# A transformer block on one core: wider steps in the first MLP product, thirteen shared buffers, another order of the residual's statistics, fewer opening products

## The chip, the cores and the metric

The kernel runs on one core of one Trainium2 chip. The time is device microseconds of one execution, and a kernel is judged by the median of several executions. The engines that matter here are PE (TensorE, matrix products), DVE (VectorE), ACT (ScalarE), POOL (GpSimd) and SP (SyncE, which here only issues transfers). Each has a queue of its own, and they wait for each other through semaphores.

## The reference

One sequence of 2048 tokens, width D = 576, 32 heads of 18 features, MLP width 4608:

```python
    def _A_ref(x, wqkv, w_phi, wo):
        ...
        phi_q = jnp.concatenate([_softmax(pq, axis=-1), _softmax(-pq, axis=-1)], axis=-1)
        phi_k = jnp.concatenate([_softmax(pk, axis=-1), _softmax(-pk, axis=-1)], axis=-1)
        kv = jnp.einsum("bhsf,bhsd->bhfd", phi_k, v)
        z  = jnp.einsum("bhsf->bhf", phi_k)
        num = jnp.einsum("bhqf,bhfd->bhqd", phi_q, kv)
        den = jnp.einsum("bhqf,bhf->bhq", phi_q, z)[..., None] + 1e-6
        o = num / den
        return (...)(o, 0, 2, 1, 3).reshape(B, S, D) @ wo
    def _B_ref(x, w1, b1, w2, b2):
        y = _layernorm(x, axis=-1)
        h = _gelu(jnp.einsum("bsd,df->bsf", y, w1) + b1)
        return jnp.einsum("bsf,fd->bsd", h, w2) + b2
    x = A_x
    h = x + _A_ref(_layernorm(x, axis=-1), A_wqkv, A_w_phi, A_wo)
    h2 = h + _B_ref(_layernorm(h, axis=-1), B_w1, B_b1, B_w2, B_b2)
```

So there is a layer norm, a linear attention with softmax features, a residual, a second layer norm, and an MLP with a second residual. All inputs are bf16.

## The kernel before, in words

The 2048 tokens are 16 tiles of 128, taken as 8 pairs. `NS` is 8 and `TB` is 256: one pair of tiles. The order of every engine's instructions is the order in which the source issues them (`manual_schedule` over all five engines), so a line that stands earlier in the source stands earlier in its engine's queue. Nothing is planned by a cost model.

**The front** (L705 to L1053) is a list of calls written out by hand. It opens with `warm(20)`: twenty products of the identity with 512 columns, whose result nobody reads. It folds the feature weights into the query and key weights (`flip_mm`, `fold_k_mm`, with casts on ACT by `fold_k_ev`), copies half of the value weights to the other partitions on POOL (`copy_values`, L162), and runs keys, values and queries for all pairs. Query features are kept as `phiq`, eight buffers.

**The MLP** is eight blocks, `mlp(s_)` for `s_` in 0 to 7, each over one pair of tiles:

- `up` is the first product. Its contraction over 576 is cut into nine steps of two halves of 64 rows. The two matmuls of a step take separate halves of the array and run side by side. One `pair(...)` is 18 matmuls (nine steps) of 256 columns into two PSUM buffers of the pool `acc` (six buffers). Eighteen pairs make one `up`, 324 matmuls on L1075. ACT applies GELU to both buffers (L1096) and writes `h`.
- `down` is the second product: per tile and half of the output 36 matmuls of 288 columns (L1117), 144 in a block. DVE adds the bias and residual (L1121), and a transfer on SP writes the tile out.
- Between them stands what feeds later blocks. `norm_q` sums and divides the query features (DVE L460 and L462, POOL L466); `turn_q` transposes them by two transfers on SP (L494) into `phiT`; `combine` makes ten matmuls on them (L588) and a division on DVE (L598, L601); `turn` transposes the result (L618) into `oT`; `enter` does the attention's output product (36 matmuls, L635), the residual and its statistics on DVE (L648, L649), the second normalisation (POOL L239, DVE L243), and transposes each tile (L677) into `ln2T`, the moving operand of a later `up`.

`at` holds calls that are issued at a given pair of `up` or at a given matmul of `down`. In the block `s_ = 1`, `norm_q` of pair 3 ends and `turn_q(3)` follows at pair step 3 of `up`; `enter(2)` follows `up`; `combine(6)` stands at matmul 30 of `down`, `leave(3)` (that is `combine(7)` and `turn(3)`) at 76, and the two halves of `norm_q(4, ...)` at 90 and 110. The later blocks do the same one pair further on, as long as pairs remain.

`ln2T` is two buffers of 256 tokens that alternate. The MLP's `h` takes the four buffers of `lnt_pool`, `phiq` and `phiT` rotate through nine of `ex_pool`.

Of the kernel before, what the change touches and what calls it, by code (L numbers as in the profile page):

```python
# [8 lines left out]
P = 128  # L9
# [13 lines left out]
NM = FF // P  # L23
# [16 lines left out]
def kernel(  # L40
# [82 lines left out]
    def region(at, n):  # L123
        return shared[:, at : at + n]
# [9 lines left out]
    ln2T = [  # L134
        region(4 * PW + i * KC * TB, KC * TB).rearrange("p (c t) -> p c t", c=KC)
        for i in range(2)
    ]
# [121 lines left out]
    def chunks(t):  # L259
        return xh[:, t, :].rearrange("p (c k) -> p c k", k=KH)  # L260

    lnT = [
        lnt_pool.tile([P, 2, KC, P], BF16, name="lnT", tag="lnT") for _ in range(NT // 4)
    ]
    moments = {}

# [182 lines left out]

    def query_exp(p, i):  # L450
        if p not in phiq:
            phiq[p] = ex_pool.tile([P, 2, PW], BF16, name="phiq", tag="ex")
        exponentials("q", phiq[p], p, i)

    def part_of(dst, i):
# [33 lines left out]
            query_weigh(p, i, a, pool)  # L489

    def turn_q(p):
        phiT[p] = ex_pool.tile([P, 2, KC, P], BF16, name="phiT", tag="ex")
        for a in range(2):
            nc.sync.dma_start_transpose(phiT[p][:, a, :, :], phiq[p][:, a, :])  # L494

    left = list(range(NT))

# [73 lines left out]
        )  # L571

    products = {}

    def combine_mm(t, part=None, home=None):
        p, a = divmod(t, 2)
        if not part:
            products[t] = (home or pn_pool).tile(
                [P, 2, 512], FP32, name="pn", tag="two" if home else "pn"
            )  # L580
        pn = products[t]
        for w in range(*((0, KC) if part is None else ((0, 5), (5, KC))[part])):
            h0, h1 = FIRST[w], FIRST[w] + COUNT[w]
            for b in range(2):
                lo, hi = max(h0, b * HH), min(h1, (b + 1) * HH)
                if lo >= hi:
                    continue
                nc.tensor.matmul(  # L588
                    pn[:, b, (lo - b * HH) * VW : (hi - b * HH) * VW],
                    phiT[p][:, a, w, :], kvm[:, w, (lo - h0) * VW : (hi - h0) * VW],  # L590
                    start=(w == 0 or (b == 1 and lo == HH)),
                    stop=(w == KC - 1 or (b == 0 and hi == HH)), skip_group_check=True,
                )

    def divide(t):
        rec = small.tile([P, 2, HH], FP32, name="rec", tag="rec")
# [42 lines left out]
        flight["a", p, i] = pa  # L639

    def residual_add(p, i, a):
        if (p, a) not in gathered:
            gathered[p, a] = small.tile(
                [P, 2, nc.vector.BN_STATS_DIM], FP32, name="st2", tag="st2"
            )
        t = 2 * p + a
        cs = slice(i * HALF, (i + 1) * HALF)
        nc.vector.tensor_tensor(xh[:, t, cs], flight["a", p, i][a], xh[:, t, cs], ALU.add)  # L648
        nc.vector.bn_stats(gathered[p, a][:, i, :], xh[:, t, cs])  # L649

    def second(t):
        p, a = divmod(t, 2)
# [4 lines left out]
    def residual(p, banks):  # L657
        for i in range(2):
            residual_mm(p, i, banks())
            for a in range(2):  # L660
                residual_add(p, i, a)
                if i:
                    second(2 * p + a)

# [5 lines left out]
        return ln2[t % 2][:, :, :, :].rearrange("p c two k -> p (c two k)")  # L670

    def place2(t):
        s_, i_ = divmod(t, TPS)
        return ln2T[s_ % 2][:, :, i_ * P : (i_ + 1) * P]

    def turn2(t):
        nc.sync.dma_start_transpose(place2(t), rows2(t))  # L677
# [332 lines left out]
    query_mm(1, 0)  # L1010
    residual_mm(0, 1, double_bank())
    residual_add(0, 1, 0)
    residual_add(0, 1, 1)
    query_exp(1, 0)
    query_mm(6, 1)
    query_exp(6, 1)
# [3 lines left out]
    query_mm(1, 1)  # L1020
    query_exp(1, 1)
    residual_add(0, 0, 0)
    second(0)
    residual_add(0, 0, 1)
    close_keys()
    query_mm(2, 1)
    second(1)
# [24 lines left out]
    close_weights()  # L1052
    load_w2(0, 3)  # L1053
    hb_pool = side_pool("hb_pool", 1)
    tt_pool = side_pool("tt_pool", 1)
    psA.close()

    acc = ctx.enter_context(
# [5 lines left out]
            acc.tile([P, HALF], FP32, name="pa", tag="acc")[:, :] for _ in range(2)  # L1064
        ]

    def up(s_, at, first=0):
        x = ln2T[s_ % 2]
        h1 = [lnt_pool.tile([P, KC, TB], BF16, name="h1", tag="lnT") for _ in range(4)]

        def pair(ph, p_, cols):
            for c in range(KC):
                for half in range(2):
                    rows = slice(half * KH, (half + 1) * KH)
                    nc.tensor.matmul(  # L1075
                        ph[half][:, cols],
                        w1[p_ // 9][rows, c, p_ % 9 * P : (p_ % 9 + 1) * P], x[rows, c, cols],
                        start=(c == 0), stop=(c == KC - 1),
                    )

        def banks_of():
            return [acc.tile([P, TB], FP32, name="ph", tag="acc") for _ in range(2)]

        begun = [banks_of() for _ in range(first)]
        for p_ in range(first):
            pair(begun[p_], p_, slice(0, P))
            if p_ == 0:
                yield
        for p_ in range(NM // 2):
            if p_ in at:  # L1090
                at[p_]()
            ph = begun[p_] if p_ < first else banks_of()
            pair(ph, p_, slice(P if p_ < first else 0, TB))
            for half in range(2):
                m = p_ + half * NM // 2
                nc.scalar.activation(  # L1096
                    h1[m // 9][:, m % 9, :], ph[half][:, :], AF.Gelu_apprx_tanh,
                    bias=b1col[:, m : m + 1], scale=1.0,
                )
        yield h1  # L1100

    def down(s_, h1, at):
        k = 0
        for i_ in range(TPS):
            t = s_ * TPS + i_
            hb = hb_pool.tile([P, D], FP32, name="hb", tag="hb")
            nc.gpsimd.tensor_tensor(hb[:, :], xh[:, t, :], b2bc[:, :], ALU.add)  # L1107
            ot = tt_pool.tile([P, D], BF16, name="ot", tag="ot")
            for i in range(2):
                cs = slice(i * HALF, (i + 1) * HALF)  # L1110
                po = acc.tile([P, HALF], FP32, name="po", tag="acc")
                for n in range(NM):
                    m = n // 2 + n % 2 * NM // 2
                    if k in at:
                        at[k]()
                    k += 1
                    nc.tensor.matmul(  # L1117
                        po[:, :], h1[m // 9][:, m % 9, i_ * P : (i_ + 1) * P], w2[m // 18][:, m % 18, cs],
                        start=(n == 0), stop=(n == NM - 1),
                    )  # L1120
                nc.vector.tensor_tensor(ot[:, cs], po[:, :], hb[:, cs], ALU.add)  # L1121
            nc.sync.dma_start(out_v[:, t, :], ot[:, :])

    def enter(a):
        residual(a, two_banks)
# [6 lines left out]
        combine(2 * p + 1)  # L1132
        turn(p)

    def mlp(s_):
        a, b, c = s_ + 1, s_ + 2, s_ + 3
        rises, falls = {}, {}
        if s_ == 0:
            rises = {
                6: lambda: [load_w2(1, n) for n in range(6)],  # L1140
                15: lambda: combine(2 * a),
                17: lambda: turn_q(b),
            }
        if s_ == 1:
            rises[3] = lambda: (norm_q(b, 1), turn_q(b))
        rise = up(s_, rises, 1 if s_ == 0 else 0)
        if s_ == 0:
            turn2_mm(1, pn_pool)
            next(rise)
            for part in range(2):  # L1150
                turn2_ev(1, part, dve)
            for q in (a, b):
                for i in range(2):
                    norm_q(q, i)
                if q == a:
                    turn_q(q)
        h1 = next(rise)
        if s_ == 0:
            falls = {
                0: lambda: leave(a), 64: lambda: enter(a), 84: lambda: combine(2 * b),  # L1160
                96: lambda: norm_q(c, 0), 118: lambda: leave(b),
            }
        else:
            if a < NS:
                enter(a)
            if b < NS:
                falls[30] = lambda: combine(2 * b)
                falls[76] = lambda: leave(b)
            if c < NS:
                falls[90] = lambda: norm_q(c, 0)  # L1170
                falls[110] = lambda: (norm_q(c, 1), turn_q(c))
        down(s_, h1, falls)

    for s_ in range(NS):
        mlp(s_)
    ordered.close()


# [28 lines left out]
```

## Time and profile before

| what | value |
|---|---|
| median of 3 runs | 400.38 us (400.46, 400.38, 397.94) |
| the profiled execution's own time | 397.7 us |
| its span | 396.0 us |
| PE busy | 386.7 us, 98% of the span |
| PE's share of the chain that ended last | 92% |
| granted clock of PE | 1.0 |

The page gives busy time by engine, the span in 40 slices, the chain of work that ended last (followed back from the last instruction), and groups of instructions by line and shape. Mean times of single matmuls include the overlap with their neighbours. The duration of a stretch in the chain, divided by its count, is therefore the better measure of what one matmul costs. In the timeline a row merges neighbours of one kind; PEld is the loading of weights for a matmul, which runs beside PE.

### The profile page before, as it was taken

To read this page: it belongs to the slowest core of one execution; us is meant where nothing else is said; L and a number is where in the kernel's file an instruction comes from. 1 tells how busy PE (TensorE), PEld (TensorE's weight loads), DVE (VectorE), ACT (ScalarE), POOL (GpSimd) and SP (SyncE) were. 2 spreads that over 40 slices of the span, in tenths; PEclk is the share of its full clock that TensorE was granted. 3 is DMA by queue.
4 is the path that set the end of the run, shared out by engine and by line. 5 is a ranking of instruction groups with operands and counts; after the bars stand their busy time and mean duration, and the time that the engine had idled before them with its cause. 6 is when DMAs were issued, how large, how long until landed. Compare 5 with 4: busy or idle time off the path is not lost.

```text
span 396.0 us, 12120 instructions
## 1 busy us (share of the span) xinstructions
PE 386.7 (98%) x5424; PEld 318.2 (80%) x5424; DVE 163.7 (41%) x347; ACT 186.6 (47%) x399; POOL 124.0 (31%) x148
## 2 busy tenths in 40 slices
PE   8899999889999999999999999999999999999996
PEld 4687777679878888888888888888887888778874
DVE  5999894485248026403630462065107200600000
ACT  3978887678500850184028303820481058007700
POOL 7999998019004203400340133023202100211010
PEclk9999999999999999999999999999999999999999
DMA  8999869998924605510460053005300400210000
GB/s 221 190 173 175 196 113 165 213 238 222 280 48 84 99 2 76 74 33 2 80 81 22 3 102 78 4 2 105 78 2 18 89 17 2 41 37 17 2 17 15
DMA packets 72163, 33.83 MB, mean 85 GB/s; under 512 B 58786, under 2 KB 69296, under 8 KB 72112
## 3 DMA queue, kind: packets, MB, share of 16 engines
q1 hardware_dynamic: 71760, 32.75, 41.9%
q8 instruction: 42, 0.69, 0.7%
q10 hardware_dynamic: 288, 0.30, 0.3%
q14 instruction: 9, 0.07, 0.1%
q0 software_dynamic: 64, 0.02, 0.0%
HBM read 16.53 MB, written 2.36 MB: 48 GB/s over the span
## 4 chain that ended last, share of the span: by engine, by line
PE 92%; POOL 3%; DVE 2%; DMA 1%; issue 1%; POOLq 0%
PE ph L1075 36%; PE po L1117 36%; PE pk L409 7%; PE pa L635 4%; PE pv L409 4%; PE acc_kv L503 2%; PE pn L588 2%; DMA w<-in_A_w_phi_dram 1%; POOL wv L162 1%; POOL vals L209 1%; POOL rs L285 1%; PE pW L379 0%; DVE shared L243 0%; POOL w L201 0%; DVE ob L601 0%
## 5 line engine op out<-in xcount | busy, mean ns | idle before, releaser
L1096 ACT ACTIVATE h<-ph,b1col 128x256 bf16<-128x256 f32 x288 | 120.7, 470 | 166.9 <-PE ph L1075 149.0
L1117 PE MATMUL po<-w,h 128*128 128x288 bf16 x1152 | 144.7, 287 | 0.0
L1075 PE MATMUL ph<-shared,w 64*128 64x256 bf16 (+1 forms) x2610 | 143.3, 269 | 0.0
L1075 PEld LDWEIGHTS <-w 64*128 64x128 bf16 x2610 | 127.6, 94 | 15.0 <-issue 1.7
L1117 PEld LDWEIGHTS <-h 128*128 128x128 bf16 x1152 | 111.2, 98 | 29.3 <-issue 1.9
L239 POOL TENSOR_TENSOR rs<-va,mhalf 128x1 f32<-128x1 f32 x16 | 8.8, 549 | 171.4 <-DVE va L237 171.4
L648 DVE TENSOR_TENSOR xh<-pa,xh 128x288 bf16<-128x288 f32 x32 | 14.3, 447 | 114.9 <-PE pa L635 114.9
L409 PEld LDWEIGHTS <-lnT 64*128 64x128 bf16 x864 | 42.0, 94 | 10.4 <-issue 0.3
L1121 DVE TENSOR_TENSOR ot<-po,hb 128x288 bf16<-128x288 f32 x32 | 14.6, 456 | 80.5 <-PE po L1117 79.7
L466 POOL TENSOR_TENSOR phiq<-phiq,rk 128x576 bf16<-128x576 bf16 x32 | 36.4, 1162 | 21.6 <-DVE rk L462 16.3
L1107 POOL TENSOR_TENSOR hb<-xh,b2bc 128x576 f32<-128x576 bf16 x16 | 20.4, 1273 | 62.8 <-DVE ot L1121 61.1
L466 POOL TENSOR_TENSOR phik<-phik,rk 128x576 bf16<-128x576 bf16 x32 | 36.4, 1163 | 1.7 <-PE pv L409 0.9
L460 DVE TENSOR_REDUCE sk<-phik 128x64 f32<-128x1152 bf16 x16 | 21.2, 1323 | 5.2 <-ACT phik L431 5.2
L431 ACT ACTIVATE phiq<-pk 128x576 bf16<-128x576 f32 x32 | 18.7, 650 | 6.6 <-PE pk L409 6.6
L460 DVE TENSOR_REDUCE sk<-phiq 128x64 f32<-128x1152 bf16 x16 | 21.3, 1334 | 0.2 <-ACT phiq L431 0.2
L409 PE MATMUL pv<-wv,lnT 64*128 64x288 bf16 x288 | 20.6, 283 | 0.1
L431 ACT ACTIVATE phik<-pk 128x576 bf16<-128x576 f32 x32 | 18.8, 653 | 3.2 <-PE pk L409 3.2
L409 PE MATMUL pk<-shared,lnT 64*128 64x288 bf16 x288 | 19.8, 283 | 0.0
L409 PE MATMUL pk<-wqp,lnT 64*128 64x288 bf16 x288 | 19.7, 283 | 0.0
L635 PE MATMUL pa<-wo,shared 64*128 64x288 bf16 x288 | 19.1, 283 | 0.0
L462 DVE RECIPROCAL rk<-sk 128x64 f32<-128x64 f32 x32 | 17.7, 553 | 1.5
L635 PEld LDWEIGHTS <-shared 64*128 64x128 bf16 x288 | 14.0, 94 | 3.6 <-issue 0.2
(70 smaller groups left out, 194.5 us busy)
## 6 DMA issues: line engine op xcount, KB each, us to landing
w<-in_B_w_dram SPq DMA_DIRECT2D x24, 432.0 KB, 7.9
out_dram<-ot SPq DMA_DIRECT2D x16, 144.0 KB, 1.7
xh<-in_A_x_dram SPq DMA_DIRECT2D x3, 576.0 KB, 6.9
wo<-in_A_wo_dram SPq DMA_DIRECT2D x4, 324.0 KB, 6.4
wv<-in_A_wqkv_dram SPq DMA_DIRECT2D x2, 324.0 KB, 8.4
w<-in_A_wqkv_dram SPq DMA_DIRECT2D x4, 157.5 KB, 9.5
wqp<-wqp SPq DMA_DIRECT2D x2, 288.0 KB, 3.9
w<-in_A_wqkv_dram SPq DMA_DIRECT2D x1, 322.0 KB, 4.9
```

Of the source, the lines that this page charges most:

```text
L409: nc.tensor.matmul(dst[:, a, 0:HALF], lhs[rows, c, :], w[rows, slot, i * HALF : (i + 1) * HALF], start=(n == 0), stop=(n == KC - 1),)
L431: nc.scalar.activation(rows[:, :, i * HH : (i + 1) * HH, s, :], flight[key, p, i][:, :, 0:HALF].rearrange("p a (h f) -> p a h f", f=DH), A ...
L460: nc.vector.tensor_reduce(sk[:, :, :], part_of(dst, i), AX.X, ALU.add)
L462: nc.vector.reciprocal(rk[:, :, :], sk[:, :, :])
L466: eng.tensor_tensor(part, part, flight["r" + key, p, i][:, a, :].rearrange("p (h o) -> p h o", o=1).to_broadcast([P, NH, DH]), ALU.mult,)
L635: nc.tensor.matmul(pa[a], oT[p % 2][rows, c, :], wo[rows, c, cs], start=(c == 0), stop=(c == KC - 1),)
L648: nc.vector.tensor_tensor(xh[:, t, cs], flight["a", p, i][a], xh[:, t, cs], ALU.add)
L1075: nc.tensor.matmul(ph[half][:, cols], w1[p_ // 9][rows, c, p_ % 9 * P : (p_ % 9 + 1) * P], x[rows, c, cols], start=(c == 0), stop=(c == KC ...
L1096: nc.scalar.activation(h1[m // 9][:, m % 9, :], ph[half][:, :], AF.Gelu_apprx_tanh, bias=b1col[:, m : m + 1], scale=1.0,)
L1107: nc.gpsimd.tensor_tensor(hb[:, :], xh[:, t, :], b2bc[:, :], ALU.add)
L1117: nc.tensor.matmul(po[:, :], h1[m // 9][:, m % 9, i_ * P : (i_ + 1) * P], w2[m // 18][:, m % 18, cs], start=(n == 0), stop=(n == NM - 1),)
L1121: nc.vector.tensor_tensor(ot[:, cs], po[:, :], hb[:, cs], ALU.add)
```

## The change

The source differs in these places, and only in these:

- `warm(20)` becomes `warm(13)`.
- The pools `lnt_pool` and `ex_pool` are replaced by thirteen buffers `home0` to `home12` of the same total size, given out by `take` and returned by `leave_home` in the order of the source. Transposed input, `phiq`, `phiT` and `h` all live there.
- `residual_add` is split: the addition stays, the statistics move to `residual_stats`. In `residual` both tiles' additions now stand ahead of both tiles' statistics. The buffers of the statistics are four instead of three.
- `ln2T` is one region of 512 tokens with four places, tile `t` at place `t % 4`.
- The MLP is five blocks: pairs 0 and 1 alone, then pairs 2 and 3, 4 and 5, 6 and 7 together. In a double block `up` works on 512 columns: 18 pairs of 18 matmuls for four tiles, GELU on 128x512, `h` in nine buffers, four values of `m` in each. `down` makes 288 matmuls.
- The calls between are placed anew. The second block's `up` holds the rest of `norm_q(3)`, `norm_q(4)`, `norm_q(5)`, `combine(6)` and `leave(3)`; its `down` holds `enter(3)` at matmul 44 and `combine(8)` to `leave(5)` between 98 and 136. Double blocks call `enter` for both next pairs right after `up`.
- `tt_pool`, the tile on its way out, has two buffers instead of one.

```diff
-    lnt_pool = ctx.enter_context(tc.tile_pool(name="lnt_pool", bufs=4))
-    ex_pool = ctx.enter_context(tc.tile_pool(name="ex_pool", bufs=9))
...
+    homes = [persist.tile([P, 2 * PW], BF16, name=f"home{i}", tag=f"home{i}") for i in range(13)]
+    vacant = list(range(13))
+    taken = {}
+    def take(key):
+        taken[key] = vacant.pop(0)
+        return homes[taken[key]][:, :]
+    def leave_home(key):
+        vacant.append(taken.pop(key))
...
+    ln2T = region(4 * PW, 2 * KC * TB).rearrange("p (c t) -> p c t", t=2 * TB)
...
-        phiT[p] = ex_pool.tile([P, 2, KC, P], BF16, name="phiT", tag="ex")
+        phiT[p] = take(("phiT", p)).rearrange("p (a c k) -> p a c k", a=2, k=P)
         for a in range(2):
             nc.sync.dma_start_transpose(phiT[p][:, a, :, :], phiq[p][:, a, :])
+        leave_home(("phiq", p))
...
         nc.vector.tensor_tensor(xh[:, t, cs], flight["a", p, i][a], xh[:, t, cs], ALU.add)
-        nc.vector.bn_stats(gathered[p, a][:, i, :], xh[:, t, cs])
...
             for a in range(2):
                 residual_add(p, i, a)
+            for a in range(2):
+                residual_stats(p, i, a)
                 if i:
                     second(2 * p + a)
...
-    warm(20)
+    warm(13)
...
-    tt_pool = side_pool("tt_pool", 1)
+    tt_pool = side_pool("tt_pool", 2)
...
+    def up(p0, n, at, first=0):
+        width = n * TB
+        base = p0 % 2 * TB
+        per = 2 * PW // width
+        h1 = [take(("h1", p0, i)) for i in range((NM + per - 1) // per)]
+        def hidden(m):
+            return h1[m // per][:, m % per * width : (m % per + 1) * width]
...
                     nc.tensor.matmul(
-                        ph[half][:, cols],
-                        w1[p_ // 9][rows, c, p_ % 9 * P : (p_ % 9 + 1) * P], x[rows, c, cols],
+                        ph[half][:, lo:hi],
+                        w1[p_ // 9][rows, c, p_ % 9 * P : (p_ % 9 + 1) * P],
+                        ln2T[rows, c, base + lo : base + hi],
                         start=(c == 0), stop=(c == KC - 1),
                     )
...
-            return [acc.tile([P, TB], FP32, name="ph", tag="acc") for _ in range(2)]
+            return [acc.tile([P, 2 * TB], FP32, name="ph", tag="acc") for _ in range(2)]
...
+    def second_block():
+        hidden = next(up(1, 1, {
+            3: lambda: (norm_q(3, 1), turn_q(3)),
+            5: lambda: norm_q(4, 0),
+            7: lambda: (norm_q(4, 1), turn_q(4)),
+            10: lambda: combine(6),
+            12: lambda: leave(3),
+            13: lambda: norm_q(5, 0),
+            14: lambda: (norm_q(5, 1), turn_q(5)),
+        }))
+        enter(2)
+        down(1, 1, hidden, {
+            44: lambda: enter(3), 98: lambda: combine(8), 110: lambda: leave(4),
+            122: lambda: combine(10), 136: lambda: leave(5),
+        })
+    def double_block(p):
+        rises, falls = {}, {}
+        if p == 2:
+            rises = {
+                3: lambda: norm_q(6, 0), 6: lambda: (norm_q(6, 1), turn_q(6)),
+                9: lambda: norm_q(7, 0), 12: lambda: (norm_q(7, 1), turn_q(7)),
+            }
+            falls = {
+                110: lambda: combine(12), 130: lambda: leave(6),
+                150: lambda: combine(14), 170: lambda: leave(7),
+            }
+        hidden = next(up(p, 2, rises))
+        if p + 2 < NS:
+            enter(p + 2)
+            enter(p + 3)
+        down(p, 2, hidden, falls)
+    first_block()
+    second_block()
+    for p in (2, 4, 6):
+        double_block(p)
```

More of the change, by code (lines that the diff above doesn't have):

```diff
@@ L262 @@
     lnT = [
-        lnt_pool.tile([P, 2, KC, P], BF16, name="lnT", tag="lnT") for _ in range(NT // 4)
+        take(("lnT", i)).rearrange("p (a c k) -> p a c k", a=2, k=P) for i in range(NT // 4)
     ]
@@ L451, in query_exp @@
         if p not in phiq:
-            phiq[p] = ex_pool.tile([P, 2, PW], BF16, name="phiq", tag="ex")
+            phiq[p] = take(("phiq", p)).rearrange("p (a f) -> p a f", a=2)
         exponentials("q", phiq[p], p, i)
@@ L593, in combine_mm @@
                 )
+        if part != 0:
+            combined.add(t)
+            if {2 * p, 2 * p + 1} <= combined:
+                leave_home(("phiT", p))
     def divide(t):
@@ L672, in place2 @@
     def place2(t):
[L673 to L674 removed]
+        return ln2T[:, :, t % 4 * P : (t % 4 + 1) * P]
     def turn2(t):
@@ L1065, in two_banks, with pair @@
         ]
[L1067 to L1071, printed above, removed]
+    def up(p0, n, at, first=0):
[5 more added lines that the diff above has]
+            return h1[m // per][:, m % per * width : (m % per + 1) * width]
+        def pair(ph, p_, lo, hi):
             for c in range(KC):
@@ L1092, in up @@
             ph = begun[p_] if p_ < first else banks_of()
-            pair(ph, p_, slice(P if p_ < first else 0, TB))
+            pair(ph, p_, P if p_ < first else 0, width)
             for half in range(2):
@@ L1096, in up, with down @@
                 nc.scalar.activation(
-                    h1[m // 9][:, m % 9, :], ph[half][:, :], AF.Gelu_apprx_tanh,
+                    hidden(m), ph[half][:, 0:width], AF.Gelu_apprx_tanh,
                     bias=b1col[:, m : m + 1], scale=1.0,
                 )
-        yield h1
-    def down(s_, h1, at):
+        yield hidden
+    def down(p0, n, hidden, at):
         k = 0
-        for i_ in range(TPS):
-            t = s_ * TPS + i_
+        for i_ in range(2 * n):
+            t = 2 * p0 + i_
             hb = hb_pool.tile([P, D], FP32, name="hb", tag="hb")
@@ L1111, in down @@
                 po = acc.tile([P, HALF], FP32, name="po", tag="acc")
-                for n in range(NM):
-                    m = n // 2 + n % 2 * NM // 2
+                for j in range(NM):
+                    m = j // 2 + j % 2 * NM // 2
                     if k in at:
@@ L1133, in leave, with first_block @@
         turn(p)
-    def mlp(s_):
-        a, b, c = s_ + 1, s_ + 2, s_ + 3
+    for i in range(NT // 4):
+        leave_home(("lnT", i))
+    def first_block():
+        rise = up(0, 1, {
+            6: lambda: [load_w2(1, n) for n in range(6)],
+            15: lambda: combine(2),
+            17: lambda: turn_q(2),
+        }, 1)
+        turn2_mm(1, pn_pool)
+        next(rise)
+        for part in range(2):
+            turn2_ev(1, part, dve)
+        for q in (1, 2):
+            for i in range(2):
+                norm_q(q, i)
+            if q == 1:
+                turn_q(q)
+        down(0, 1, next(rise), {
+            0: lambda: leave(1), 64: lambda: enter(1), 84: lambda: combine(4),
+            96: lambda: norm_q(3, 0), 118: lambda: leave(2),
+        })
```

62 lines of the change are left out of this document (18 added, 44 removed).

## The prediction

> **What bounds the kernel now.** I read the page's busy times first, then the shares of the chain that ended last.
>
> ```profile
> span 396.0 us, 12120 instructions
> PE 386.7 (98%) x5424; PEld 318.2 (80%) x5424; DVE 163.7 (41%) x347; ACT 186.6 (47%) x399; POOL 124.0 (31%) x148
> ...
> PE 92%; POOL 3%; DVE 2%; DMA 1%; issue 1%; POOLq 0%
> ```
>
> PE is the only engine near its span, but a busy PE need not be an efficient one. So I went to the chain in order of time, where start, length and count of each stretch stand.
>
> ```profile
> 19.45 1.39 POOL wv L162
> 20.84 0.04 issue
> 20.89 2.36 PE pv L409 x35
> ...
> 27.01 1.21 PE pv L409 x18
> 28.22 1.10 PE pk L409 x18
> ...
> 86.76 15.07 PE ph L1075 x288
> ...
> 126.62 17.79 PE ph L1075 x324
> 144.41 2.20 PE pa L635 x36
> 146.61 3.78 PE po L1117 x30
> 150.40 0.37 PE pn L588 x10
> 150.76 5.64 PE po L1117 x46
> ...
> 374.56 17.76 PE po L1117 x144
> 392.32 0.02 issue
> 392.34 0.46 DVE ot L1121
> ```
>
> The reader is to see two regimes. Up to 20.84 the chain is POOL's copies of the value weights. From 86.76 to 392.32 every stretch is PE's, each beginning where the last ended: 305.6 us without one wait. In this part only the length of PE's own stream counts, and whatever else is moved must merely not be late.
>
> **The wide step.** A step is one pair of half-height matmuls side by side. A stretch that follows full-height matmuls is 0.11 longer (1.21 against 1.10 for the same 18 at 27.01 and 28.22): the price of changing over. So one `up` is 17.79 - 0.11 = 17.68 us in 162 steps, 109.1 ns for 256 columns. No step of 512 columns is in the trace; the nearest are the opening products, full-height matmuls of 512 columns. These are their weight loads, which keep the pace of the products:
>
> ```profile
> 1.82 0.15 PEld L233 LDWEIGHTS <-ident 128*128 128x128 bf16 x1 [0.28 <-issue]
> ...
> 4.38 0.15 PEld L233 LDWEIGHTS <-ident 128*128 128x128 bf16 x1 [0.28 <-issue]
> ...
> 4.78 2.26 PEld L233 LDWEIGHTS <-ident 128*128 128x128 bf16 x11 [0.25 <-issue]
> ```
>
> At first they stand (4.38 - 1.82) / 6 = 427 ns apart, later (2.26 - 0.10) / 10 = 216 ns: PE starts slow and doubles its pace at about 4.8 us. At the fast pace 256 more columns cost 216 - 109.1 = 106.9 ns, so 109.1 ns are 106.9 of columns and 2.2 of fixed cost per step. Three double blocks replace 6 x 162 = 972 steps of 256 by 486 of 512: 486 fixed costs go, 486 x 2.2 = **1.1 us**. The bounds: nothing is saved if the cost is wholly in proportion to columns (a step of 218.2 ns); the double, 2.1 us, if wide steps lose the fixed cost altogether (214 ns). I take 1.1, because 216 is a measured row of that width.
>
> [...]
>
> The 0.11 changeovers: half-height stretches in the MLP before are two in the first `up` (parted by `combine(2)`), `enter(1)`, and seven later `up` with the `enter` that adjoins them: ten. After: two, `enter(1)`, three in the second `up` (parted by `combine(6)` and `combine(7)`), `enter(3)`, three double blocks: ten. No gain, no loss. All other matmuls stay in number and size.
>
> **GELU.** ACT works beside PE:
>
> ```profile
> L1096 ACT ACTIVATE h<-ph,b1col 128x256 bf16<-128x256 f32 x288 | 120.7, 470 | 166.9 <-PE ph L1075 149.0
> ```
>
> Two GELUs per pair take 0.94 us against 0.98 of PE, a thin cover. On 512 columns one costs between 0.47 and 0.94 us, so two cost at most 1.88 against 9 x 0.216 = 1.94: still covered, at worst as thinly as today. Cover that never was missed is worth nothing when it grows, so I count 0.
>
> **Seven opening products less.** Seven at the fast pace are 1.5 us. These rows are the front of PE:
>
> ```profile
> 7.16 0.31 PEld L348 LDWEIGHTS <-w 128*128 128x128 bf16 x2
> ...
> 7.37 1.79 PE L348 MATMUL pX<-ident,w 128*128 128x128 bf16 x25
> ...
> 15.49 0.68 PE L321 MATMUL pT<-ident,shared 128*128 128x128 bf16 x9 [1.17 <-ACT shared L372]
> 16.10 2.38 PE L409 MATMUL pk<-shared,lnT 64*128 64x288 bf16 x36
> ...
> 20.52 2.73 PE L409 MATMUL pv<-wv,lnT 64*128 64x288 bf16 x36
> ```
>
> The folding of weights (L348 on) could start earlier by up to 1.5 us, but PE then stands for ACT (1.17 us at 15.49) and again at 20.52, where one matmul is issued and the other 35 wait until 20.89 for POOL's copy. POOL's chain waits for no PE work. So in the profiled execution the saving disappears in the wait at 20.89: 0. The bounds are 0 and the case in which PE doubles its pace later than here, the second rival. The timed runs lie up to 2.8 us above the profiled one, and this edit is the only one that can reach into the front; for them I take 0.5 us, nearer to the profile's 0.
>
> **What moves.** In the second block more is asked of DVE, POOL and SP during `up`. The same stage before:
>
> ```profile
> 127.31 1.34 DVE L460 TENSOR_REDUCE sk<-phiq 128x64 f32<-128x1152 bf16 x1
> 128.68 0.55 DVE L462 RECIPROCAL rk<-sk 128x64 f32<-128x64 f32 x1
> 129.31 2.28 POOL L466 TENSOR_TENSOR phiq<-phiq,rk 128x576 bf16<-128x576 bf16 x2 [2.40 <-DVE rk L462]
> ...
> 130.50 2.73 SPq L494 DMA_TRANSPOSE phiT<-phiq  x2
> ...
> 145.55 0.46 DVE L648 TENSOR_TENSOR xh<-pa,xh 128x288 bf16<-128x288 f32 x1 [16.31 <-PE pa L635]
> 146.04 0.46 DVE L649 BATCH_NORM_STATS2 st<-xh 128x6 f32<-128x288 bf16 x1
> ...
> 149.86 2.01 DVE L243 TENSOR_SCALAR shared<-xh,mv,rs 128x576 bf16<-128x576 bf16 x4
> ...
> 150.97 3.41 SPq L677 DMA_TRANSPOSE shared<-shared  x2
> ```
> ```profile
> DMA to landing us min/median/max: 3.3/4.4/5.9
> ...
> shared<-shared SPq DMA_TRANSPOSE x14, 3.3
> ```
>
> (The last two rows are the times to landing of the transfers into `phiT`, and of those of `enter`, the median.) DVE had 16.31 us of idleness there, so the moved `norm_q` halves (1.9 us of DVE, 2.3 of POOL each) fit. Four of them after the first make 7.6 on DVE and 9.2 on POOL. The tightest due times:
>
> - `combine(6)` at pair 10: 126.62 + 9.9 = 136.5. The transposed features are issued at 130.50 and land by 136.4 even with the slowest 5.9; the median 4.4 leaves 1.6 us. `combine(7)` needs the second transfer, issued about 1.4 later, and stands 2.4 later.
> - On SP `turn(3)` and `turn_q(5)` follow `turn_q(4)`. `norm_q(5)` can start only after the division of `combine(7)`, about 140.7; its last POOL product ends near 147, and `turn_q(5)` leaves SP about 148.4. The transposes of `enter(2)` behind it were issued from 150.97: 2.5 us to spare. POOL's power for `enter(2)`, due at 148.7, also finds POOL free.
> - `enter(3)` at matmul 44 of `down`: its transposes land some 1.2 (18 matmuls) + 6.3 (from the addition at 145.55 to the end of L243, 149.86 + 2.01) + 1.4 (the second issue) + 3.3 = 12.2 us later; 2.3 for its own matmuls, 100 x 0.123 and four `combine` of 0.37 make 16.1 until the next `up`.
> - Two `enter` in a row need eight accumulation buffers of six. `down`'s first buffer is free once the second half's first addition is done: 1.1 for 18 matmuls, two additions and two statistics of 0.46 and that addition, 3.4 us in all; PE takes 4 x 1.1 = 4.4 to get there.
>
> The `home` buffers bring waits of GELU on earlier readers, but those are PE's matmuls of the block before, which are ahead in PE's own queue, or transfers landed long ago. The split statistics, `tt_pool` and the single `ln2T` lie under the same PE stream. All of this I cost at 0; the price if a cover is gone is PE standing still for what is late, one for one.
>
> **Sum.** Profiled: 397.7 - 1.1 = 396.6 us. Against the median shown: 400.38 - 1.1 - 0.5 = 398.8 us, or 0.4% less. About 1% is what a measurement of this kernel can tell from no change.
>
> **Rivals.**
>
> 1. *Wide steps save nothing* (or the change does nothing to the bound): a step of 218.2 ns, time 399.9 to 400.4. For it: that 512-column row is of full-height matmuls, and two weight loads per step are at work here too. Against it: a half-height stretch of 288 columns, 1.10 / 9 = 122.2, and a full-height one, 5.64 / 46 = 122.6, cost the same. Chance 0.13.
> 2. *PE's pace doubles late in most runs.* If it came 3.4 us later, as long again as from 1.42 to 4.8, eight more of the twenty products would run at 427, and the folding would begin 8 x 0.211 = 1.7 us later; with ACT behind it, the keys would come 1.7 later and overrun POOL's 20.89 by 1.7 - 0.37 = 1.3 us. Thirteen products end by 1.42 + 13 x 0.427 = 7.0 us even so, just ahead of the data at 7.16. Such runs gain 1.3 + 1.1: 398.0, and up to 396.5 if the front explains the whole 2.7 us above the profile. For it: two of three runs stand 2.5 us above the third. Against it: the one profile has the early pace. Chance 0.22. [...]
> 3. *The crowded second block makes PE wait*, the case on the slower side. Its place is `combine(6)` at pair 10: when `turn_q(3)` lands after 136.5, PE stands, `combine(7)`, `turn(3)` and `enter(3)` slip with it. Its price is the lateness, one for one; from 1.6 us of lateness over the median landing the gain is being eaten, from 2.7 us the kernel is slower than before, and with 6 to 7 us (a DVE or POOL that is held through the combines) it is over 1% slower: 404.5. Against it: DVE's idleness above. Chance 0.13.
> 4. *PE's pace drops* between thirteen products, ending near 5.9, and the data at or before 7.16, a gap under 1.3 us; with another slow start the folding loses up to 1.7, less the 0.37 in the wait at 20.89 and the 1.5 by which it starts earlier: about 0, with the wide steps 399.3. Against it: after the 1.17 us gap at 15.49, 36 matmuls took 2.38, full pace. Chance 0.06.
>
> **How the numbers follow.** My forecast, 398.8, has 0.46. The range must take in rival 1 (400.4) and rival 2 (down to 396.5), and a lateness of 1 to 3 us from rival 3; the low end adds the second 1.1 of the step's lower bound to rival 2's: 395.4. The high end, 401.6, leaves out the worst half of rival 3. [...] Slower by over 1%: most of rival 3, and a stall I have not seen: 0.11. The rest, 0.76, lies within 1%.
>
> **What would show it.** In the chain after, the double blocks' `ph` stretches at 35.1 us for 324 matmuls, 162 x 0.216 + 0.11 (35.5 would be rival 1); PE without a break from the first `up` to the last; GELU on 512 columns below 0.94; POOL's copy again ahead of the first values near 20.9. A wait of PE on a transfer into `phiT` or `ln2T`, or on `pa` additions, would be rival 3. I would be wrong above all if side-by-side halves of 512 columns hinder each other, since then 486 steps pay.

## The result, and the profile after

| | before | after |
|---|---|---|
| median of 14 runs each, same chip | 399.4 us (397.48 to 401.17) | 396.32 us (396.02 to 397.75) |
| ratio | 1 | 0.9931, 95% interval 0.9914 to 0.9948 |
| profiled execution, its span | 397.7, 396.0 | 397.03, 395.0 |
| PE busy in it | 386.7 us | 385.4 us |
| granted clock in it | 1.0 | 0.996 |

The change makes the kernel 0.7% faster. That is inside the 1% of the forecast and inside its range, but more than the 0.4% at its centre. The two medians are 3.1 us apart, where the forecast had 1.6; and the kernel before now stands at 399.4 us over 14 runs, not at the 400.38 over three from which the forecast started. Spread counts too: the executions before lie within 3.7 us, those after within 1.7, and ten of the fourteen within 0.4.

The profile shows one part of this at once, and the other only if one looks at the clock. First the chain that ended last of the kernel after, in order of time (start, length, what), from the first `up` on.

```profile
87.11 15.07 PE ph L1100 x288
102.18 0.48 PE pn L596 x10
...
162.67 0.37 PE pn L596 x10
...
164.50 0.46 PE pn L596 x10
...
166.43 0.46 PE pn L596 x10
...
169.95 35.07 PE ph L1100 x324
205.02 4.41 PE pa L647 x72
...
246.29 35.07 PE ph L1100 x324
281.36 4.41 PE pa L647 x72
285.77 35.39 PE po L1143 x288
321.16 35.07 PE ph L1100 x324
356.23 35.40 PE po L1143 x288
391.63 0.02 issue
391.65 0.46 DVE ot L1147
```

From 87.11 to 391.63 it is PE's stream without a break, as before: 304.52 us against 305.56 (86.76 to 392.32). The 1.04 us is what the MLP gained in these two profiles. Each wide `up` takes 35.07 us; two narrow ones took 2 x 17.79. The calls placed anew brought no wait of a matmul on `phiT`, `ln2T` or an addition. In the second block only two `combine` at 164.50 and 166.43 take 0.46 us instead of the 0.37 of 162.67. The division that frees their buffer had ended before (at 164.28 for the first), so why they take longer stays open.

GELU on the wide tile, by groups of line and shape (count, busy time, mean ns):

```profile
L1122 ACT ACTIVATE home<-ph,b1col 128x512 bf16<-128x512 f32 x108 | 68.4, 684 | 142.3 <-PE ph L1100 99.6 <-issue 42.8
L1100 PE MATMUL ph<-shared,w 64*128 64x512 bf16 x972 | 105.4, 376 | 0.0
```

Two GELUs are 1.37 us beside 1.94 of PE, where it had been 0.94 beside 0.98. The cover grew, but it had not been missed before, so nothing was gained by it.

The first `up` begins later than in the profile before (87.11 against 86.76), although PE started its folding earlier. The timeline of PE's front in the kernel after (start, length, line, what, count, wait before it), and the windows of one microsecond (the figure behind the five engines is PE's granted clock, as a share of full speed), show why:

```profile
1.42 4.41 PE L239 MATMUL pw<-ident 128*128 128x512 bf16 x13 [1.42 <-POOL ident masks.py:199]
6.21 1.80 PE L354 MATMUL pX<-ident,w 128*128 128x128 bf16 x25 [0.37 <-DMA w<-in_A_wqkv_dram]
...
14.62 1.14 PE L327 MATMUL pT<-ident,shared 128*128 128x128 bf16 x9 [0.97 <-DVE shared L303]
15.69 3.50 PE L415 MATMUL pk<-shared,home 64*128 64x288 bf16 x36
...
14.00:15.00 1.00, 0.38 (x4) 0.38 (x5) 1.00 (x4) 0.78 (x2) 0.81 (x3) 0.80 1.28 255
15.00:16.00 1.00, 1.00 (x12) 0.72 (x11) 0.97 (x4) 0.54 (x1) 0.94 (x3) 0.50 1.33 225
16.00:17.00 1.00, 1.00 (x12) 0.66 (x10) 0.95 (x3) 1.00 (x2) 1.00 (x2) 0.50 1.00 168
17.00:18.00 1.00, 1.00 (x12) 0.64 (x10) 0.92 (x4) 0.09 (x1) 0.96 (x1) 0.50 0.19 36
18.00:19.00 1.00, 1.00 (x20) 0.77 (x16) 0.18 (x1) 0.93 (x2) 0.86 (x2) 0.99 0.63 122
```

In this execution PE ran at half pace from about 14.6 to 18.0. The same 36 key matmuls that had taken 2.38 us take 3.50, the nine transposes 1.14 instead of 0.68. This execution is one of the few that have it: of the fourteen, two show a granted clock of 0.996 or less, and the ten at 1.0 have a median span of 394.25 us against 395.2 for these two. So the profiled execution understates the gain, and the experiments are read with the span and clock of every execution beside the medians.

### The profile page after: what moved, and what is told of

It reads as the page before. It is cut to its first block, busy times and chain, and to the rows that moved or that the text cites. A ratio compares the mean times of both kernels' runs of the same rounds, so it can differ in the third digit from the quotient of the medians.

```text
span 395.0 us, 10113 instructions
## 1 busy us (share of the span) xinstructions
PE 385.4 (98%) x4445; PEld 269.3 (68%) x4445; DVE 162.0 (41%) x347; ACT 164.4 (42%) x291; POOL 123.9 (31%) x148
## 4 chain that ended last, share of the span: by engine, by line
PE 94%; DVE 4%; DMA 1%; issue 0%; SPq 0%
PE po L1143 36%; PE ph L1100 36%; PE pk L415 8%; PE pv L415 5%; PE pa L647 5%; PE acc_kv L510 2%; PE pn L596 2%; DMA w<-in_A_wqkv_dram 1%; DVE st L282 1%; PE pT L327 1%; PE pW L385 0%; DVE shared L249 0%; DVE shared L303 0%; DVE ob L613 0%; DVE w L360 0%
## 5 line engine op out<-in xcount | busy, mean ns | idle before, releaser
L1122 ACT ACTIVATE home<-ph,b1col 128x512 bf16<-128x512 f32 (+1 forms) x180 | 98.6, 599 | 170.7 <-PE ph L1100 102.2
L1143 PE MATMUL po<-w,home 128*128 128x288 bf16 x1152 | 144.0, 286 | 0.0
L1100 PE MATMUL ph<-shared,w 64*128 64x512 bf16 (+2 forms) x1638 | 141.9, 331 | 0.0
L1143 PEld LDWEIGHTS <-home 128*128 128x128 bf16 x1152 | 111.5, 98 | 29.2 <-issue 1.6
L1100 PEld LDWEIGHTS <-w 64*128 64x128 bf16 x1638 | 79.9, 94 | 60.4 <-issue 0.9
L1147 DVE TENSOR_TENSOR ot<-po,hb 128x288 bf16<-128x288 f32 x32 | 14.6, 455 | 111.9 <-PE po L1143 111.7
L415 PEld LDWEIGHTS <-home 64*128 64x128 bf16 x864 | 41.2, 95 | 12.0 <-issue 0.2
L472 POOL TENSOR_TENSOR home<-home,rk 128x576 bf16<-128x576 bf16 x32 | 36.1, 1165 | 26.6 <-DVE rk L468 21.2
L466 DVE TENSOR_REDUCE sk<-home 128x64 f32<-128x1152 bf16 x16 | 21.1, 1317 | 0.2 <-ACT home L437 0.2
L415 PE MATMUL pk<-shared,home 64*128 64x288 bf16 x288 | 20.8, 293 | 0.0
L415 PE MATMUL pv<-wv,home 64*128 64x288 bf16 x288 | 20.2, 283 | 0.0
L415 PE MATMUL pk<-wqp,home 64*128 64x288 bf16 x288 | 19.7, 283 | 0.0
```

The costliest lines, as they stand in the source:

```text
L415: nc.tensor.matmul(dst[:, a, 0:HALF], lhs[rows, c, :], w[rows, slot, i * HALF : (i + 1) * HALF], start=(n == 0), stop=(n == KC - 1),)
L466: nc.vector.tensor_reduce(sk[:, :, :], part_of(dst, i), AX.X, ALU.add)
L472: eng.tensor_tensor(part, part, flight["r" + key, p, i][:, a, :].rearrange("p (h o) -> p h o", o=1).to_broadcast([P, NH, DH]), ALU.mult,)
L1100: nc.tensor.matmul(ph[half][:, lo:hi], w1[p_ // 9][rows, c, p_ % 9 * P : (p_ % 9 + 1) * P], ln2T[rows, c, base + lo : base + hi], start=(c ...
L1122: nc.scalar.activation(hidden(m), ph[half][:, 0:width], AF.Gelu_apprx_tanh, bias=b1col[:, m : m + 1], scale=1.0,)
L1143: nc.tensor.matmul(po[:, :], hidden(m)[:, i_ * P : (i_ + 1) * P], w2[m // 18][:, m % 18, cs], start=(j == 0), stop=(j == NM - 1),)
```

## The experiments

Two theories stood against each other. *Front theory*: 1 us comes from the wide steps, and the rest from the opening products, which in most executions of before cost more than in its profiled one. *MLP theory*: the rest comes from the new order in the MLP. Each kernel was timed beside the kernel before, whose medians in the three sets of runs were 399.84 to 399.89 us.

### One part alone: fewer opening products

```diff
-    warm(20)
+    warm(13)
```
(in the kernel before)

> The kernel before with 13 opening products instead of 20, nothing else. Front theory (the gain beyond the wide steps comes from fewer opening products, whose time in most executions is longer than in the profiled one): about 1.6 us faster than before, ratio 0.996, with the spread of its executions narrowed to that of the changed kernel (about 1.7 us instead of 3.7). MLP theory (the gain beyond the wide steps comes from the new order of the MLP): ratio 1.000 within 0.001 and the spread of before.

Measured: 398.2 us, ratio 0.997 (0.9951 to 0.999): 1.7 us faster than before. The spread narrowed to 2.4 us, not to 1.7. Front theory holds in size. MLP theory's 1.000 lies outside the interval, whose end touches the margin of 0.001 that it had allowed itself.

### The other part alone: 20 opening products in the changed kernel

```diff
-    warm(13)
+    warm(20)
```

> The changed kernel with 20 opening products again. Front theory: only the wide steps are left, 1.05 us, ratio 0.997, and the wide spread of before. MLP theory: the whole gain stays, ratio 0.993.

Measured: 398.39 us, ratio 0.9961 (0.9941 to 0.9981). That is 2.1 us above the changed kernel's 396.32 of the earlier runs, and 1.9 above the 396.54 that the kernel of the fourth experiment, whose time is the changed kernel's, took on the same chip. MLP theory's 0.993 lies outside the interval. The spread is 2.4 us, more than the changed kernel's 1.7 but not the wide one of before that was expected (4.4 us beside this kernel). The weight loads of its opening products, with the windows in which its clock is under 1:

```profile
6.09 0.15 PEld L239 LDWEIGHTS <-ident 128*128 128x128 bf16 x1 [0.28 <-issue]
6.52 1.40 PEld L239 LDWEIGHTS <-ident 128*128 128x128 bf16 x7 [0.28 <-issue]
...
16.00:17.00 1.00, 0.62 (x9) 0.56 (x9) 1.00 (x3) 0.71 (x2) 0.85 (x3) 0.88 1.12 194
17.00:18.00 1.00, 1.00 (x10) 0.58 (x10) 0.97 (x5) 1.00 (x2) 1.00 (x2) 0.50 0.65 114
...
20.00:21.00 1.00, 1.00 (x18) 0.76 (x16) 0.26 (x1) 0.71 (x2) 0.94 (x2) 0.91 1.11 202
```

And its chain, from the start:

```profile
1.42 7.00 PE pw L239 x20
8.42 1.64 PE pX L354 x25
...
11.35 3.92 ACT shared L378 x8
...
16.38 0.82 PE pT L327 x9
17.20 3.79 PE pk L415 x35
```

Two things are to be seen. The pace doubled at about 6.5 us, not 4.8, so that the twenty products ended at 8.4 and set the end of the chain: POOL's copies, which had led it up to 20.84 in the profile of before, are gone from it. And the pace fell again from 16.8 to 20.2, into the keys. The first `up` begins at 88.96, 2.5 us after that of the next kernel, whose pace doubled at 4.0 and did not fall.

### The wide steps undone

```diff
-            pair(ph, p_, P if p_ < first else 0, width)
+            lo = P if p_ < first else 0
+            while lo < width:
+                hi = min(width, (lo // TB + 1) * TB)
+                pair(ph, p_, lo, hi)
+                lo = hi
```

> The changed kernel with each pair of a double block done as nine steps of the first 256 columns and then nine of the second, so that the fixed cost of a step is paid again 486 times; buffers, GELU and order stay. Both theories: 486 x 2.2 = 1.1 us slower than the changed kernel, ratio 0.996; the stretch of one double block's first product 35.36 to 35.5 us against 35.07. If wide steps are worth nothing by themselves: ratio 0.993.

Measured: 397.66 us, ratio 0.9949 (0.9933 to 0.9966), 1.1 to 1.3 us slower than the changed kernel by the same two comparisons. In the chain (of this kernel) a double block's `up` is

```profile
86.44 15.07 PE ph L1100 x288
...
169.28 35.48 PE ph L1100 x648
...
321.30 35.48 PE ph L1100 x648
```

35.48 us against 35.07, three times 0.41 = 1.23 us: 2.5 ns for each of 486 steps. The wide steps are worth what they were forecast to be.

### Statistics between the additions, as before

```diff
             for a in range(2):
                 residual_add(p, i, a)
-            for a in range(2):
                 residual_stats(p, i, a)
```

> The changed kernel with each tile's statistics right behind its addition again, as before. Front theory: no change against the changed kernel, ratio 0.993; PE would find its buffers in time in either order (by rows of before, the first buffer of the second product is free 3.9 us after the first output matmul at the latest, needed at 4.4). MLP theory: some of the 1.6 us comes back, ratio up to 0.997, with waits of PE on additions into xh between the two products of the double blocks.

Measured: 396.54 us, ratio 0.9925 (0.9901 to 0.9948); the chain from the first `up` is 304.51 us (87.23 to 391.74), as in the changed kernel. This part of the change is worth nothing by itself.

### More, and fewer, opening products

```diff
-    warm(13)
+    warm(30)
```
and, in a second kernel, `warm(8)`.

> The changed kernel with 30 opening products. Front theory: the weights' folding is held up until the products end, at 1.42 + 8 x 0.427 + 22 x 0.216 = 9.6 us if PE doubles its pace early and 1.42 + 16 x 0.427 + 14 x 0.216 = 11.3 us if late. The keys follow about 8.9 us after that (17.13 - 8.25 in the changed kernel with 20), 18.4 to 20.2, and only 16.1 + 0.4 are covered by POOL's copies: 1.9 to 3.7 us slower than the changed kernel, 398.2 to 400.1 us, ratio 0.996 to 1.000. MLP theory: 0.993, since the products would lie beside the loads and POOL's copies.

> The changed kernel with 8 opening products, which end near 4.9 us, 1.3 us ahead of the weights. Front theory: nothing gained over 13, since the weights' landing at 6.2 and POOL's copies hold the front: ratio 0.993, 396.2 us. If the products are needed for PE's full pace in the folding (it stays at half pace there): the 90 folding matmuls fall behind ACT's casts, keys up to 3 us later, up to 2.6 us slower, ratio 0.9995.

Measured with 30: 399.67 us, ratio 1.0001 (0.9984 to 1.0018), 3.2 us slower than the kernel with 8 on the same chip, and 3.3 than the changed one; the keys start at 18.52 in the profile. Products that PE still has to do when the weights have landed are paid, and the whole gain of the change is eaten by seventeen of them. MLP theory's 0.993 is far outside.

Measured with 8: 396.49 us over 4 runs, ratio 0.9911 (0.9888 to 0.9935), the same as with 13. PE's front with 8:

```profile
6.05 2.85 PE L354 MATMUL pX<-ident,w 128*128 128x128 bf16 x25 [1.04 <-DMA w<-in_A_wqkv_dram]
8.70 1.17 PE L327 MATMUL pT<-ident,shared 128*128 128x128 bf16 x9
...
15.04 0.68 PE L327 MATMUL pT<-ident,shared 128*128 128x128 bf16 x9 [0.78 <-DVE shared L303]
15.65 2.38 PE L415 MATMUL pk<-shared,home 64*128 64x288 bf16 x36
```

The first folding matmuls run at half pace (2.85 us instead of 1.80), and so do nine transposes (1.17 instead of 0.66). Yet the keys start at 15.65: PE still waits 0.78 us for DVE ahead of them, and POOL's copies, which end at 20.36, hold the values back in any case. With 8 nothing was gained over 13, and nothing lost.

### Both parts undone

This kernel has the wide steps undone as above and `warm(20)`.

> The changed kernel with both parts undone: 20 opening products, and each double pair in two lots of 256 columns. What is left of the change are buffers, places of the calls, statistics after additions. Front theory: as the kernel before, ratio 1.000 within 0.0015, 399.9 us. MLP theory: 0.996 or less.

Measured: 399.18 us, ratio 0.998 (0.9964 to 0.9996). This is neither of the two: 0.7 us below before, with an interval that just leaves out 1. From the first `up` on its profile is no shorter than that of before (305.75 us against 305.56), so the MLP's order is not where it comes from. It shows in both kinds of executions: those at a clock of 0.996 or less have a median span of 397.9 us against 398.5 for the kernel before on the same chip, those at 1.0 have 395.8 (three) against 397.4 (seven).

The other kernels leave a remainder of the same size. In the first of these sets of runs the changed kernel (with its statistics between) is 3.33 us below before; undoing the wide steps gives back 1.12 of it, and fewer opening products in the kernel before gain 1.67; 0.54 belongs to neither. So about 0.5 us, hardly more than these runs can tell, comes from something else in the change, and neither theory has it. As the MLP is no shorter, it should lie ahead of the first `up`, where the change also put other buffers under the keys, values and queries and moved the statistics of the first pair. No run here tests these by themselves, so what it is stays open.

### The half pace before the keys: filling the wait

```diff
+    def fill(n):
+        for _ in range(n):
+            nc.tensor.matmul(
+                acc_kv[:, 1, 476:512], ident[:, :], ident[:, 0:36],
+                start=False, stop=False, skip_group_check=True,
+            )
...
     fold_k_mm(5)
+    fill(24)
```

> The changed kernel with 24 products of 36 columns into unused columns of an accumulation buffer, put where PE waits before the keys (after the last folding matmuls). In the profiles of the changed kernel PE's granted clock fell to 0.5 for 3.3 us right after this wait. If PE's low activity there sets off the fall: no execution with a clock under 1, and none above 396.6 us; the fill itself lies in a wait of 1 us and costs 0 to 0.3. If not: about 4 of 14 executions stay 1 us longer at a clock of 0.994 to 0.999. The median moves little in either case: ratio 0.993.

> The changed kernel with 20 opening products and the 24 narrow products in PE's wait before the keys. With 20 products alone the granted clock of 8 of 12 executions was 0.996 or less (PE at half pace for 3.3 us). If PE's thin activity in the folding and the wait behind it sets off the fall: at most 2 of 12 at 0.996 or less, the executions that had it 1.0 to 1.7 us shorter, median 397.0 to 397.5 us. If the fall has another cause: more than half at 0.996 or less, median as with 20 products alone, 398.4 us.

(The second kernel has `warm(20)` besides.) Measured in the changed kernel: 397.36 us, ratio 0.9939 (0.9923 to 0.9955), 0.9 us above the kernel with 8 products on the same chip, so *slower*, with no execution at 0.996 or less of six, and three at 0.999. That half of the expectation that concerns time was wrong. The keys start at 15.07, the earliest of all, but the chain at 47.67 holds a transfer that it did not hold before,

```profile
47.67 5.62 DMA home<-shared
53.28 0.05 issue
53.33 3.48 PE pk L422 x54
```

the transpose of normalised input, for which PE stands 0.91 us. That is about what the kernel lost. The transfer itself is slow here: it lands in 5.6 us, where it took 3.8 in the profile of the changed kernel (issued at 48.72). The profile of the other kernel with the fill has the same:

```profile
48.77 5.74 DMA home<-shared
54.52 0.05 issue
54.56 3.48 PE pk L422 x54
```

There PE stands 0.88 us. Why the transfer takes longer with the fill is not known, and whether every execution meets it is not shown; both profiles do, and all six executions took 397.04 us or more.

Measured with 20 products and the fill: 397.82 us, ratio 0.9956 (0.9936 to 0.9977). The falls are gone: none of 12 executions at 0.996 or less, against 8 of 12 with 20 products and no fill. (The two profiles with the fill show 0.998 and 0.999 over the whole execution, but 1.00 in their windows from 13 to 22 us, where the falls were.) So 24 narrow products that compute nothing, put into PE's wait, prevent the fall. This fits the half of the expectation in which PE's thin activity there sets it off; in what way it does so no run shows. The median is only 0.6 us lower, less than forecast, and the two ratios, 0.9956 and 0.9961, cannot be told apart: the 0.88 us that PE stands for the transfer eat most of what the missing falls save.

### POOL's part of the front

```diff
-    ones()
     fold_k_mm(8)
...
     copy_values(1, 0, gps)
+    ones()
```

> The changed kernel with POOL's fill of the ones among the values (2.3 us, on the chain that sets the front) moved behind the last copy of the value weights. If POOL's copies are what holds the front once the opening products are out of the way: PE finds them ready and the wait of 0.3 to 0.6 us ahead of the first values' second half goes: 0.3 to 0.5 us faster than the changed kernel, 395.8 to 396.0 us. If PE's own front (folding, casts, keys) holds it: no change, 396.3 us.

Measured: 397.07 us, ratio 0.9951 (0.9929 to 0.9974), 0.7 us above the changed kernel's 396.32; one of the twelve executions took 400.37 at a clock of 0.991. Both expectations missed. POOL's wait where the ones had stood and its last copy in this kernel, and PE's wait at the sums over keys (timelines):

```profile
11.05 0.19 POOL L289 TENSOR_SCALAR va<-mv 128x2 f32<-128x2 f32 x1 [1.57 <-DVE mv L283]
...
18.80 1.38 POOL L168 COPY wv<-wv 64x1440 bf16<-64x1440 bf16 x1
...
27.05 0.37 PE L510 MATMUL acc_kv<-vals,phik 128*128 128x76 bf16 x5 [0.79 <-POOL phik L472]
```

and POOL's last copy in the kernel with the wide steps undone, whose front is the changed one's:

```profile
19.14 1.38 POOL L168 COPY wv<-wv 64x1440 bf16<-64x1440 bf16 x1
```

2.3 us of work taken from ahead of the copies brought the last one only 0.34 us forward, and that is no more than profiles differ anyway (18.76 in the changed kernel with the fill, where the ones still stand ahead). The first row shows why: POOL spends 1.57 of the freed time waiting for DVE's statistics, which its next step needs. And the 2.3 us put behind it push the weighting of the key features back, for which PE then stands 0.79 us. None of these kernels clearly beats the changed one.

## Why the prediction was right, and where it was short

- **Wide steps: right in mechanism and nearly in size.** Forecast 486 x 2.2 = 1.1 us; undone by themselves they cost 1.23, 2.5 ns a step. Rival 1 (nothing saved, 35.5 for an `up`) is out: a wide `up` took 35.07.
- **Changeovers and moved calls: right up to 0.2.** With the wide steps undone the time from the first `up` on is 305.74 us (86.44 to 392.18) against 305.56 before. The two `combine` that are 0.09 longer than the others, in this kernel too, would make up that difference; the forecast had costed the moved calls at 0. Rival 3, a late `phiT`, did not occur.
- **GELU, `home` buffers, statistics, the second output buffer: 0, as forecast.** For GELU and the statistics this is shown (684 ns under the bound of 940; the statistics put back). For the buffers it rests on PE's unbroken stream, which speaks for the MLP only: about 0.5 us of the gain belongs to neither part that was undone, and the prediction's sentence that the opening products are the only edit that can reach into the front is not borne out.
- **Seven opening products: the step that was short.** The forecast gave them 0 in the profiled execution and 0.5 us in the median; taken out of the kernel before they gained 1.7, and put back into the changed one they cost 1.9 to 2.1 us. The working took the profile of before for the usual case, and it is a rare one. Of 73 executions of before that were timed beside the experiments, 38 had a granted clock of 0.996 or less, with a median span of 398.5; 26 had 1.0, with 396.85; the profiled one had 1.0 and 396.0, and four of the 73 were as short. Rival 2 had the mechanism for part of this: a late doubling holds up the folding, which starts at 7.37 with the pace doubled at 4.8 (the profile of before), and at 8.25 with it doubled at 6.5 (20 products in the changed kernel). During the opening products the doubling came between about 4.0 and 6.5 us, not as late as the 8.2 that the rival had priced; with 8 products it came only behind the first folding matmuls. The rest is the falls, which the rival did not have. How the two divide is known by profiles only: the first `up` begins at 88.38 with 20 products and the fill, at 86.44 in the kernel with the wide steps undone; take off the 0.88 for the transfer, and about 1.1 us are left for the products and their late doubling, near the rival's 1.3. The fall made the first 36 key matmuls 1.1 to 1.5 us longer (3.50 in the changed kernel and 3.85 with 20 products, against 2.38).
- **The data were nearer than the prediction read.** It took 7.16 for the time at which the weights are there. In that row no wait stands; it is where PE's own queue came to them, behind the twenty products. In the profiles in which PE waits for them, with 8 or 13 products, the folding starts between 6.05 and 6.83. So even thirteen products, if all were at the slow pace, would end at 7.0, behind the data.
- **Rival 4 had the right event on the wrong side.** It feared that *thirteen* products would let PE's pace fall. The pace does fall, but chiefly with *twenty*: in 14 of 24 executions of the two kernels with the new MLP and 20 products, in 5 of 42 of the four kernels with 13 and nothing else done to the front, in none of 10 with 30 and none of 4 with 8. And it does not fall in the gap behind the products but 8 to 9 us later, in the wait before the keys. The argument used against it, a gap of 1.17 us in the profile of before without a fall, was one instance of a matter of chance.
- **The sum.** Forecast 1.1 + 0.5 = 1.6 us; the medians moved by 3.1, the MLP's part 1.04. The range held it because rival 2 had been taken in down to 396.5 and the step's lower bound below that. A result within 1% had been given 0.76, one over 1% faster 0.13. Part of the hit is luck: against the 400.38 us from which the forecast counted, 396.32 would be 1.0% less, at the edge of the band that it had called likeliest; it is 0.7% because the kernel before came out at 399.4.
- **The signs.** PE's unbroken stream, the 35.07 us of a wide `up` and GELU's 684 ns came as forecast. POOL's copy ahead of the first values is not in the chain of the profile after, because the fall made PE later than POOL; it is there in the kernel with the wide steps undone, where the copy ends at 20.52 and the values follow at 20.57.

## What to carry to other kernels

A profile is one execution: where runs of the same kernel spread by more than the gain looked for, ask which edits can reach into what spreads, and do not price those by the one profile. In the stretch where one engine's stream was unbroken, a sum of fixed costs per instruction was good to a few tenths of a microsecond (1.1 forecast, 1.23 measured), and what was hidden there could be costed at nothing. Opening products were paid as soon as they outlasted the load that they fill the time for (396.49 us with 8, 396.32 with 13, 398.39 with 20, 399.67 with 30); here they are better counted for the slow pace of 427 ns than for the fast one of 216. An edit that repairs one thing can slow another: read the whole chain again, as with the fill.

## What the runs showed of the hardware that was not expected

- PE's half pace before the keys came, in each of four profiles that have it, 10.2 to 10.3 us after the doubling of the pace, and lasted 3.4 us: 4.4 and 14.6 in the changed kernel (ended 18.0), 6.5 and 16.8 with 20 products (ended 20.2), 4.4 and 14.7 with the statistics between (ended 18.2), 6.1 and 16.3 with both parts undone (ended 19.7). In the profile of the changed kernel the clock falls once more after the work is done, at 396.9. What sets these times no run shows.
- In the 3.41 us that end at the fall in the changed kernel (11.21 to 14.62), a stretch as long as the half pace, PE is busy for 2.08 us, with short products. A stretch as long in the profile of before holds 1.93 us (12.20 to 15.61), and no fall follows. So the busy time of such a stretch alone does not tell when the pace falls. Two profiles doubled their pace at 6.1; the one with 13 products had its keys at 16.05 and no fall at 16.3, the one with 20 its keys at 17.12 and the fall. More products put the thin stretch later; whether this explains the counts of falls above is not shown.
- The granted clock of the windows stood at 1.00 during the opening products (0 to 7 us in the profile of before), although their spacing was 427 ns and then 216. The fall is in that column, the slow start is not.
- 24 products of 36 columns, 0.77 us of PE, were enough to keep the pace in all 18 executions of the two kernels that had them (granted clock 0.998 or more in each).
- In the first `up`, PE sometimes stood for 0.4 to 0.75 us with nothing in the profile that it waited for (0.39 in the kernel before with 13 products, 0.75 in the changed one with 8). What it is stays open.
